# Attention and two feed-forward layers on one core: v's block sums on two column halves, and a new order of TensorE's work inside a step

## The chip, the cores and the metric

The kernel runs on one core of a Trainium2 chip. The metric is the device time of one execution in microseconds (us). Three executions of the kernel before gave 499.45 (median), 499.92 and 497.95 us. Engines are called by the names of the profile: PE is TensorE's matmuls, PEld its weight loads, DVE is VectorE, ACT is ScalarE, POOL is GpSimd, SP is the engine that issues the DMAs.

## The reference, cut to what matters

```python
# q, k, v: (2, 8, 768, 64) float32
block, window = 32, 16
k_sum = k.reshape(B, H, 24, 32, 64).max(axis=3)
v_sum = v.reshape(B, H, 24, 32, 64).mean(axis=3)
scores_l = where(|i - j| < 16, q @ k.T / 8, -1e9)
scores_s = q @ k_sum.T / 8 + log(32)
a = softmax(concat([scores_l, scores_s]))
attn = a @ concat([v, v_sum])
x = attn as (1536 tokens, 512)
h = x @ w_in;  x = (h * cos(h)) @ w_out           # 512 -> 2048 -> 512
h = x @ w_in2; x = layernorm(h * softmax(h)) * g_ln @ w_out2   # 512 -> 1024 -> 512
```

## The kernel before, in words

The 16 heads are worked in 8 pairs (n). A pair's 768 queries are cut into 12 tiles of 64, and 4 such tiles form a group G, so a pair has 3 groups and there are 24. Each tile of queries looks at a window of 96 keys and at the 24 block maxima of k, 120 columns in all. `kx` holds those columns, `qx` the scaled queries; both are copied by ACT out of one PSUM tile `qk` into which PE transposed k (L437) and q (L473).

The order of the work is written out by hand in `attention()`: a loop of 29 steps (24 groups and a lag of 5), and each engine does its instructions in just this order. In step s PE does, one after the other: some of the first feed-forward products h (`fill`, L234, in steps 15 to 18 and 20 to 28); the scores of group s+1 (`emit_s`, L501); the transposes of the softmax weights of group s-4 (`emit_t`, L538, tile `aps`); their products with v of group s-5 (`emit_av`, L556, tile `ops`); in steps 2, 5, 8, 11, 14 and 17 the transposes of the next k and q (`emit_k`, `emit_q`); in steps 1, 2, 4, 7, 10, 13, 16 and 19 the block sums of v of pairs 0 to 7 (`sum_v`, L419, tile `vsum`). Beside it, DVE does masking and maxima (L512), the softmax sums (L525, L526), the block maxima of k (L449) and the copies that lay k and q of two heads side by side (`pair_k`, `pair_q`, L375); POOL subtracts the maxima (L516) and scales by the sums (L531); ACT does the exponentials (L521), copies `aps` out as `at` (L546) and `ops` out into X (L570), `kx` and `qx`, scales `vsum` (L426, tile `vm`), and converts feed-forward weights. SP loads k, q, v and the weights, and places the scaled sums beside v, in partitions 96 to 119 of each tile of v (`place_vsum`, L430).

The block sums are a product on PE: a matrix of zeros and ones (a slice of `strip`, 96 rows by 24 columns) times a tile of v, accumulated over the 12 tiles into 24 rows of PSUM from row 96 on. The scores use 64 rows and 64 columns of PE's array for each of two heads. The transposes use the whole array (the profile shows 128*128 and 128*120), as do the products h. The products with v use 120 rows and, for the two heads in turn, the left and the right 64 columns.

After the loop the feed-forward layers follow: products y (L276) and h, 12 of 128 by 512 each, in turn, then the second layer.

Of the kernel before, what the change touches and what calls it, by code (L numbers as in the profile page):

```python
# [34 lines left out]
def fused_kernel(  # L35
# [299 lines left out]
    def attention():  # L335
        st = ExitStack()
        with st:
# [61 lines left out]
            strip = fix.tile([P, 2 * NS + 2 * (NS - 2)], F32, name="strip")  # L399
            FIRST, FINAL, MID = 0, NS, 2 * NS  # L400

            def block_columns():

                for at, row in ((FIRST, 0), (FINAL + NS - 2, WIN - QT), (MID + NS - 4, BAND)):
                    nc.vector.tensor_reduce(
                        out=strip[:, at:at + 2],
                        in_=ident[:, row:row + QT].rearrange("p (b k) -> p b k", k=BLOCK), op=ALU.add, axis=AX.X)

            def blocks_of(t):
                at = FIRST if t == 0 else FINAL if t == NT - 1 else MID + NS - 4 - 2 * t  # L410
                return strip[0:WIN, at:at + NS]

            def sum_v(n):

                o = (ps_h0 if n < 6 else ps_qk).tile(
                    [P, 512] if n < 6 else [P, 2, 2, S // 2], F32, tag="h" if n < 6 else "qk", name="vsum")
                o = o if n < 6 else o[:, 0, 0]
                for t in range(NT):
                    nc.tensor.matmul(  # L419
                        o[WIN:WIN + NS, 0:P], lhsT=blocks_of(t),  # L420
                        rhs=v_t[n][0:WIN, t].rearrange("p j d -> p (j d)"), start=(t == 0), stop=(t == NT - 1))
                vs_t[n] = o[WIN:WIN + NS, 0:P]

            def scale_v(n):
                m = io.tile([P, 2 * D], F32, tag="vm", name="vm")[WIN:WIN + NS]
# [3 lines left out]
            def place_vsum(n):  # L429
                nc.sync.dma_start(  # L430
                    out=v_t[n][WIN:WIN + NS].rearrange("p t j d -> p t (j d)"),
                    in_=vs_t.pop(n).unsqueeze(1).to_broadcast([NS, NT, 2 * D]))
# [163 lines left out]
            pair_k(1)  # L596
            pair_q(1)
            block_columns()
            emit_k(1)
            emit_q(1)  # L600
# [4 lines left out]
            for step in range(NGR + LA):  # L605
# [5 lines left out]
                fill(step)  # L611
                if step + 1 < NGR:
                    emit_s(step + 1)
                if LT <= step < NGR + LT:
                    emit_t(step - LT)
                if step >= LA:
                    emit_av(step - LA)
                if g == 2 and n + 2 < NPAIR:
                    emit_k(n + 2)
                    emit_q(n + 2)  # L620
                if step in VSUM_AT:
# [10 lines left out]
                if step < NGR:  # L632
# [335 lines left out]
```

## Time and profile before

| | |
|---|---|
| median of the three runs | 499.45 us |
| the profiled execution | 498.97 us |
| its span | 497.2 us |
| PE busy | 487.8 us (98% of the span) |
| ACT, DVE, POOL busy | 316.3, 299.9, 149.6 us |
| attention, until PE starts the products y | 0 to 109.3 us |
| share of the block sums (L419) in the chain that ended last | 4% |

The span is the time between the first and last instruction of the profiled execution; the 1.8 us to its own time lie around it. A busy PE is one that has an instruction in work: matmuls overlap, so a group of them is priced by the distance between its start and that of the next group. In the chain of waits each piece begins where the one before it released it, so its pieces give that distance directly. "x24" counts instructions: each float32 product with both operands in float32 shows as two, so 12 block sums are x24, 8 scores x16 and 8 products with v x16; transposes and products h show as one each.

### The profile page before, as it was taken

How to read it: one execution, taken by the hardware profiler on the slowest of the kernel's cores; microseconds unless marked ns; L12 is line 12 of the kernel's file. 1: busy time of each engine (PE TensorE's matmuls, PEld its weight loads, DVE VectorE, ACT ScalarE, POOL GpSimd, SP SyncE). 2: the span in 40 equal slices, each digit the busy share in tenths (PEclk: the TensorE clock that was granted, in tenths of full speed). 3: DMA queues.
4: the chain of work that ended last, by engine and by line, in shares of the span. 5: the costliest groups of instructions: out<-in, count | busy, mean ns of one | idle time of the engine just before them, and what ended most of it. 6: DMA issues, size and time to landing. Idle time of an engine off the chain costs nothing.

```text
span 497.2 us, 7856 instructions
## 1 busy us (share of the span) xinstructions
PE 487.8 (98%) x2938; PEld 400.7 (81%) x2938; DVE 299.9 (60%) x667; ACT 316.3 (64%) x540; POOL 149.6 (30%) x144
## 2 busy tenths in 40 slices
PE   6999999999999999999999999999999999999997
PEld 3888777778888888888888888888888788888886
DVE  3785775594444456465564645566476767676661
ACT  3467988673866865665566564678724876777621
POOL 1465986913422222232222221234600011110000
PEclk9999999999999999999999999999999999999999
DMA  8979852400223223322322330230001223223211
GB/s 218 233 207 267 228 130 73 140 2 0 86 87 119 90 84 105 108 86 86 116 94 84 101 112 2 85 100 28 0 1 42 81 74 96 70 64 65 63 42 44
DMA packets 58950, 46.17 MB, mean 93 GB/s; under 512 B 40352, under 2 KB 51232, under 8 KB 58912
## 3 DMA queue, kind: packets, MB, share of 16 engines
q1 hardware_dynamic: 58912, 45.67, 31.8%
q8 instruction: 23, 0.38, 0.3%
q14 instruction: 15, 0.12, 0.1%
HBM read 36.61 MB, written 3.15 MB: 80 GB/s over the span
## 4 chain that ended last, share of the span: by engine, by line
PE 92%; ACT 3%; DVE 2%; DMA 2%; SPq 0%; issue 0%; ACTq 0%
PE y L276 26%; PE h L234 26%; PE o L843 13%; PE h L729 13%; PE vsum L419 4%; PE sps L501 4%; PE aps L538 2%; PE ops L556 2%; DMA qt<-in_q_dram 2%; PE qk L473 1%; PE qk L437 1%; PE tp L777 1%; ACT kx L458 0%; ACT at L546 0%; ACT qx L487 0%
## 5 line engine op out<-in xcount | busy, mean ns | idle before, releaser
L234 PE MATMUL h<-xs,w 128*128 128x512 f32 x576 | 141.5, 392 | 0.4 <-ACT vm L426 0.4
L276 PE MATMUL y<-gs,w 128*128 128x512 f32 x576 | 138.1, 389 | 0.0
L276 PEld LDWEIGHTS y<-gs,w 128*128 128x128 f32 x576 | 108.0, 188 | 22.4
L234 PEld LDWEIGHTS h<-xs,w 128*128 128x128 f32 x576 | 107.2, 188 | 23.0 <-ACT vm L426 0.6
L187 POOL TENSOR_TENSOR w<-s,w 128x512 fp32r<-128x512 f32 x48 | 62.4, 1301 | 157.7 <-ACT w L186 134.7
L243 ACT ACTIVATE r<-h 128x512 int32<-128x512 f32 x48 | 28.7, 598 | 85.0 <-PE h L234 85.0
L248 DVE SCALAR_TENSOR_TENSOR r<-r,h 128x512 f32<-128x512 int32 x48 | 32.9, 686 | 66.8 <-ACT r L243 66.6
L843 PE MATMUL o<-w,ls 128*128 128x512 f32 (+1 forms) x312 | 67.8, 374 | 0.0
L729 PE MATMUL h<-w,xs 128*128 128x512 f32 x288 | 67.6, 390 | 0.0
L171 DVE SCALAR_TENSOR_TENSOR s<-raw 128x512 int32<-128x512 int32 x48 | 36.4, 758 | 51.0 <-ACT raw L164 43.7
L843 PEld LDWEIGHTS o<-w,ls 128*128 128x128 f32 x312 | 55.3, 188 | 10.7 <-DVE ls L819 0.4
L729 PEld LDWEIGHTS h<-w,xs 128*128 128x128 f32 x288 | 53.9, 188 | 11.1
L204 POOL TENSOR_TENSOR xs<-X,xs 128x512 fp32r<-128x512 f32 x22 | 30.7, 1405 | 35.4 <-ACT xs L203 35.4
L764 POOL TENSOR_TENSOR st<-st,mhalf 128x1 f32<-128x1 f32 x12 | 6.6, 552 | 110.1 <-DVE st L763 100.0
L253 ACT ACTIVATE r<-r,half_pi 128x512 f32<-128x512 f32 x48 | 34.4, 716 | 1.6 <-DVE r L248 1.6
L264 DVE TENSOR_TENSOR gs<-h,gs 128x512 fp32r<-128x512 f32 x48 | 32.6, 679 | 4.2 <-ACT gs L263 4.0
L516 POOL TENSOR_TENSOR sm<-sm,mx 128x480 f32<-128x480 f32 x24 | 25.7, 1070 | 27.1 <-DVE mx L512 27.1
L258 DVE TENSOR_TENSOR h<-h,r 128x512 f32<-128x512 f32 x48 | 32.8, 684 | 0.4 <-ACT r L253 0.4
L163 ACT ACTIVATE raw<-raw 128x512 f32<-128x512 f32 x48 | 31.9, 665 | 0.0
L164 ACT ACTIVATE raw<-raw 128x512 int32<-128x512 uint32 x48 | 31.8, 663 | 0.0
L186 ACT ACTIVATE w<-s 128x512 fp32r<-128x512 f32 x48 | 30.1, 627 | 1.3 <-DVE s L171 1.0
L746 ACT ACTIVATE e<-h,st 128x1024 f32<-128x1024 f32 (+1 forms) x13 | 13.6, 1049 | 26.3 <-DVE st L742 22.9
(79 smaller groups left out, 576.3 us busy)
## 6 DMA issues: line engine op xcount, KB each, us to landing
raw<-in_moe_w_in_dram SPq DMA_DIRECT2D x24, 512.0 KB, 3.5
raw<-in_moe_w_out_dram SPq DMA_DIRECT2D x24, 512.0 KB, 3.2
vt<-in_v_dram SPq DMA_DIRECT2D x16, 240.0 KB, 4.4
kt<-in_k_dram SPq DMA_DIRECT2D x8, 384.0 KB, 5.8
qt<-in_q_dram SPq DMA_DIRECT2D x8, 384.0 KB, 6.0
out_dram<-osb SPq DMA_DIRECT2D x11, 256.0 KB, 2.0
vt<-vm SPq DMA_DIRECT2D x8, 144.0 KB
vt<-in_v_dram SPq DMA_DIRECT2D x16, 48.0 KB, 3.7
```

The lines of the kernel that those rows point to most:

```text
L163: nc.scalar.activation(out=hw, in_=hw, func=AF.Prelu, scale=REBIAS, alpha=NEGATIVE)
L164: nc.scalar.activation(out=lw, in_=lw.bitcast(U32), func=AF.Copy, scale=TOP3)
L171: nc.vector.scalar_tensor_tensor(out=self.f32[i], in0=t[:, :, 1], scalar=3, in1=t[:, :, 0], op0=ALU.logical_shift_left, op1=ALU.bitwise_or)
L187: nc.gpsimd.tensor_tensor(out=w[:, 1, :], in0=f, in1=as32(w[:, 0, :]), op=ALU.subtract)
L234: nc.tensor.matmul(h, lhsT=w[:, a, f * P:(f + 1) * P], rhs=xs_of[tb, c][:, b_, :], start=(m == 0), stop=(m == 3 * KC - 1))
L248: nc.vector.scalar_tensor_tensor(out=r, in0=r.bitcast(I32), scalar=TWO_PI, in1=h_of[step], op0=ALU.mult, op1=ALU.subtract)
L253: nc.scalar.activation(out=r, in_=r, func=AF.Sin, scale=-1.0, bias=half_pi)
L258: nc.vector.tensor_tensor(out=h, in0=h, in1=r, op=ALU.mult)
L264: nc.vector.tensor_tensor(out=gs[:, 1, :], in0=r, in1=as32(gs[:, 0, :]), op=ALU.subtract)
L276: nc.tensor.matmul(y[e], lhsT=w[:, a, e * P:(e + 1) * P], rhs=gs[:, b_, :], start=(f == 0 and i == 0), stop=(f == GF - 1 and i == 2))
L729: nc.tensor.matmul(banks[n], lhsT=xs_of[NTB + t // TPB, c][:, a, t0:t0 + P], rhs=weights.done[w2i[c][n]][:, b_, :], start=(m == 0), stop=( ...
L843: nc.tensor.matmul(o, lhsT=ls_of[t][f // 4][:, a, s0:s0 + P], rhs=w[:, b_, cols], start=(f == 0 and i == 0), stop=(f == NF2 - 1 and i == 2))
```

## The change

`sum_v` now sums into two halves. Tiles 0 to 5 go through the left 64 columns of PE's array into rows 0 to 63 of PSUM, tiles 6 to 11 through the right 64 columns into rows 64 to 127, one product of each half in turn; 12 of the 64 columns of each half carry sums, the others are multiplied by zeros. `strip` is wider for that, `scale_v` scales 128 rows and not 24, and `place_vsum` issues two DMAs of 12 rows each in place of one of 24.

In a step, PE now does the scores, then `aps`, then the transposes of k and q, then `fill`, then the products with v, then the block sums. In step 0 the scores of group 1 come ahead of k and q of pair 1, and the maxima of group 0 ahead of `pair_k(1)`.

```diff
--- before.py
+++ after.py
@@ -396,40 +396,46 @@
                     )
                 v_t[n] = t
 
-            strip = fix.tile([P, 2 * NS + 2 * (NS - 2)], F32, name="strip")
-            FIRST, FINAL, MID = 0, NS, 2 * NS
+            HALF = NT // 2
+            FIRST, FINAL, MID = 0, D, 2 * D
+            strip = fix.tile([P, 3 * D + 2 * HALF], F32, name="strip")
 
             def block_columns():
 
-                for at, row in ((FIRST, 0), (FINAL + NS - 2, WIN - QT), (MID + NS - 4, BAND)):
+                for at, row in ((FIRST, 0), (FINAL + 2 * HALF - 2, WIN - QT), (MID + 2 * HALF, BAND)):
                     nc.vector.tensor_reduce(
                         out=strip[:, at:at + 2],
                         in_=ident[:, row:row + QT].rearrange("p (b k) -> p b k", k=BLOCK), op=ALU.add, axis=AX.X)
 
             def blocks_of(t):
-                at = FIRST if t == 0 else FINAL if t == NT - 1 else MID + NS - 4 - 2 * t
-                return strip[0:WIN, at:at + NS]
+                at = FIRST if t == 0 else FINAL if t == NT - 1 else MID + 2 * HALF - 2 * (t % HALF)
+                return strip[0:WIN, at:at + D]
 
             def sum_v(n):
 
                 o = (ps_h0 if n < 6 else ps_qk).tile(
                     [P, 512] if n < 6 else [P, 2, 2, S // 2], F32, tag="h" if n < 6 else "qk", name="vsum")
-                o = o if n < 6 else o[:, 0, 0]
-                for t in range(NT):
-                    nc.tensor.matmul(
-                        o[WIN:WIN + NS, 0:P], lhsT=blocks_of(t),
-                        rhs=v_t[n][0:WIN, t].rearrange("p j d -> p (j d)"), start=(t == 0), stop=(t == NT - 1))
-                vs_t[n] = o[WIN:WIN + NS, 0:P]
+                o = (o if n < 6 else o[:, 0, 0])[:, 0:P]
+                for t in range(HALF):
+                    for c in range(2):
+                        nc.tensor.matmul(
+                            o[D * c:D * c + D], lhsT=blocks_of(HALF * c + t),
+                            rhs=v_t[n][0:WIN, HALF * c + t].rearrange("p j d -> p (j d)"),
+                            start=(t == 0), stop=(t == HALF - 1))
+                vs_t[n] = o
 
             def scale_v(n):
-                m = io.tile([P, 2 * D], F32, tag="vm", name="vm")[WIN:WIN + NS]
+                m = io.tile([P, 2 * D], F32, tag="vm", name="vm")
                 nc.scalar.activation(out=m, in_=vs_t[n], func=AF.Copy, scale=1.0 / BLOCK)
                 vs_t[n] = m
 
             def place_vsum(n):
-                nc.sync.dma_start(
-                    out=v_t[n][WIN:WIN + NS].rearrange("p t j d -> p t (j d)"),
-                    in_=vs_t.pop(n).unsqueeze(1).to_broadcast([NS, NT, 2 * D]))
+                m = vs_t.pop(n)
+                for c in range(2):
+                    at = WIN + c * NS // 2
+                    nc.sync.dma_start(
+                        out=v_t[n][at:at + NS // 2].rearrange("p t j d -> p t (j d)"),
+                        in_=m[D * c:D * c + NS // 2].unsqueeze(1).to_broadcast([NS // 2, NT, 2 * D]))
 
             def transposed(t, even, odd):
 
@@ -593,11 +599,7 @@
             emit_qx(0)
             warm_up(3)
             emit_s(0)
-            pair_k(1)
-            pair_q(1)
             block_columns()
-            emit_k(1)
-            emit_q(1)
 
 
             LX, LN, LT, LA = 1, 2, 4, 5
@@ -608,16 +610,22 @@
                 ahead = n + 1 if g == 0 and n + 1 < NPAIR else 0
 
                 warm_up(IDLE[g] if step < min(FILL) else 0)
-                fill(step)
                 if step + 1 < NGR:
                     emit_s(step + 1)
+                if step == 0:
+                    emit_max(0)
+                    pair_k(1)
+                    pair_q(1)
+                    emit_k(1)
+                    emit_q(1)
                 if LT <= step < NGR + LT:
                     emit_t(step - LT)
-                if step >= LA:
-                    emit_av(step - LA)
                 if g == 2 and n + 2 < NPAIR:
                     emit_k(n + 2)
                     emit_q(n + 2)
+                fill(step)
+                if step >= LA:
+                    emit_av(step - LA)
                 if step in VSUM_AT:
                     sum_v(VSUM_AT[step])
 
@@ -629,7 +637,7 @@
                 if ahead and step:
                     emit_ksum(ahead)
                 weights.rebias()
-                if step < NGR:
+                if 0 < step < NGR:
                     emit_max(step)
                 if ahead and not step:
                     emit_ksum(ahead)
```

PE from the first scores on; `sps` are scores, `qk` the tile of the transposed k (from `kg`) and q (from `qg`). Before:

```order
L501 MATMUL sps<-kx,qx 64x120 x8
L437 MATMUL qk<-ident,kg 128x128 x6
L473 MATMUL qk<-ident,qg 128x128 x6
L501 MATMUL sps<-kx,qx 64x120 x16
L419 MATMUL vsum<-vt,strip 24x128 x12
```

With the change:

```order
L507 MATMUL sps<-kx,qx 64x120 x16
L443 MATMUL qk<-ident,kg 128x128 x6
L479 MATMUL qk<-ident,qg 128x128 x6
L507 MATMUL sps<-kx,qx 64x120 x8
L421 MATMUL vsum<-vt,strip 64x128 x12
```

The scores of group 1 moved ahead of k and q of pair 1; the block sums have 64 rows of output each and not 24.

PE from the transposes of k and q in step 14 to the block sums of step 16; `aps` are the transposed weights, `ops` the products with v, `h` the feed-forward products. Before:

```order
L437 MATMUL qk<-ident,kg 128x128 x6
L473 MATMUL qk<-ident,qg 128x128 x6
L234 MATMUL h<-xs,w 128x512 x3
L501 MATMUL sps<-kx,qx 64x120 x8
L538 MATMUL aps<-ident,sm_102 120x128 x4
L556 MATMUL ops<-at,vt 64x64 x8
L234 MATMUL h<-xs,w 128x512 x3
L501 MATMUL sps<-kx,qx 64x120 x8
L538 MATMUL aps<-ident,sm_97 120x128 x4
L556 MATMUL ops<-at,vt 64x64 x8
L419 MATMUL vsum<-vt,strip 24x128 x12
```

With the change:

```order
L443 MATMUL qk<-ident,kg 128x128 x6
L479 MATMUL qk<-ident,qg 128x128 x6
L562 MATMUL ops<-at,vt 64x64 x8
L507 MATMUL sps<-kx,qx 64x120 x8
L544 MATMUL aps<-ident,sm_102 120x128 x4
L234 MATMUL h<-xs,w 128x512 x3
L562 MATMUL ops<-at,vt 64x64 x8
L507 MATMUL sps<-kx,qx 64x120 x8
L544 MATMUL aps<-ident,sm_97 120x128 x4
L234 MATMUL h<-xs,w 128x512 x3
L562 MATMUL ops<-at,vt 64x64 x8
L421 MATMUL vsum<-vt,strip 64x128 x12
```

The transposes of k and q stand right behind `aps` and ahead of `ops`, and so do the products h, which led the step before.

## Rows read from the trace of the kernel before

**Rows 1.** The page, part 1: busy time, share of the span, instructions.

```profile
PE 487.8 (98%) x2938; PEld 400.7 (81%) x2938; DVE 299.9 (60%) x667; ACT 316.3 (64%) x540; POOL 149.6 (30%) x144
```

**Rows 2.** Busy time of each engine in stretches; first number: length of the stretch.

```profile
core 0: us, PE busy (x) PEld busy (x) DVE busy (x) ACT busy (x) POOL busy (x), PEclk, DMA share, GB/s
43.50:63.50 20.00, 19.41 (x267) 16.43 (x265) 14.17 (x57) 19.56 (x40) 16.98 (x15) 1.00 0.91 254
63.50:85.70 22.20, 21.38 (x256) 16.93 (x254) 14.10 (x62) 17.84 (x36) 17.00 (x16) 1.00 0.37 105
85.70:97.80 12.10, 12.06 (x144) 9.03 (x144) 8.71 (x44) 7.66 (x15) 11.70 (x12) 1.00 0.49 144
97.80:109.30 11.50, 10.74 (x121) 8.02 (x117) 9.61 (x19) 7.95 (x15) 1.89 (x3) 1.00 0.01 2
109.30:497.20 387.90, 384.72 (x1730) 318.95 (x1728) 225.72 (x375) 241.46 (x396) 83.31 (x70) 1.00 0.24 71
```

**Rows 3.** Chain of waits, attention: start us, us until the next piece, what.

```profile
12.74 1.79 PE sps L501 x32
14.52 2.73 PE vsum L419 x24
17.25 0.97 PE sps L501 x16
...
24.78 2.73 PE vsum L419 x24
...
29.06 0.61 PE ops L556 x16
29.68 0.81 PE qk L437 x6
30.48 0.66 PE qk L473 x6
...
63.86 0.70 PE h L234 x3
...
66.73 0.89 PE h L234 x3
```

**Rows 4.** Instructions that read v's tiles: weight loads, ns min/median/max.

```profile
L556 PEld LDWEIGHTS ops<-at,vt x384: 132/138/138, 29.0 to 109.1; 120*64 120x64 f32 x192
L419 PEld LDWEIGHTS vsum<-vt,strip x192: 98/103/103, 14.5 to 85.0; 96*24 96x24 f32 x192
```

**Rows 5.** Timeline of DVE at the start: start us, us, instruction.

```profile
9.04 0.55 DVE L375 COPY kg<-kt 128x768 f32<-128x768 f32 x1
...
10.35 0.28 DVE L512 CUSTOM_DVE_ANT_0 sm<-sps,mask 128x120 f32<-128x120 f32 x1 [0.38 <-PE sps L501]
...
11.16 0.08 DVE L512 DVE_READ_ACCUMULATOR2_ANT mx<- 128x1 f32 x1
```

**Rows 6.** Timeline of SP's issues: v of pair 2 (last), sums placed.

```profile
18.67 1.72 SPq L393 DMA_DIRECT2D vt<-in_v_dram  x1
20.49 3.04 SPq L430 DMA_DIRECT2D vt<-vm  x2
```

**Rows 7.** Loads of v issued between 18.6 and 19 us: landing.

```profile
DMA to landing us min/median/max: 4.4/4.4/4.4
```

**Rows 8.** Timeline of ACT in step 12, first piece.

```profile
52.09 0.60 ACT L546 ACTIVATE at<-aps 120x512 f32<-120x512 f32 x1
```

**Rows 9.** Timeline of PE: next aps, and late starts (in brackets).

```profile
53.41 0.65 PE L538 MATMUL aps<-ident,sm 128*120 128x128 f32 x4
...
82.58 2.80 PE L419 MATMUL vsum<-vt,strip 96*24 96x128 f32 x24 [0.50 <-ACT qx L487]
85.74 1.20 PE L234 MATMUL h<-xs,w 128*128 128x512 f32 x4 [0.36 <-ACT vm L426]
...
108.65 0.69 PE L556 MATMUL ops<-at,vt 120*64 120x64 f32 x16 [0.76 <-DVE X L568]
```

## The prediction

> **What bounds the kernel now.** I read the page first: PE is busy 98% of the span [rows 1]. Then the stretches, to see whether that holds where the change acts. From 109.3 us on, the feed-forward layers, PE is busy 384.72 of 387.90 us; the change touches nothing there, so whatever attention gains shifts that part as a whole, and what is to be found is how much earlier the products y can start than at 109.3. In attention PE is nearly full too, but between 43.5 and 63.5 us ACT is busy 19.56 of 20.00 us, between 85.7 and 97.8 POOL 11.70 of 12.10, and behind that DVE 9.61 of 11.50 [rows 2]. So PE sets the pace up to about 43 us, and later it shares it. The granted clock is full (1.00) in all of these stretches, so no piece below is one at half speed. Last, the chain of waits gives the price of each group of PE's work, from one start to the next [rows 3].
>
> **The block sums.** One pair's take 2.73 us, 24 instructions of 128 columns: 114 ns each, 0.89 ns a column. All 24 go through the same columns of the array. What work costs that alternates between two parts of the array is seen twice. 32 instructions of the scores take 1.79 us and 16 take 0.97, so 16 more cost 0.82, 51 ns each for 120 columns: 0.43 ns a column. The products with v, 16 instructions of 64 columns that alternate between the left and the right half just as the new sums do, take 0.61 us: 0.60 ns a column with their entrance (below), 0.45 without [rows 3]. So the new sums cost 24 x 128 x 0.43 = 1.31 us; at most 1.83 if the 0.60 holds for them; and 2.73 if the halves don't overlap. I take 1.31: the 120 columns of the scores are nearest to 128 in length, and the products with v come to the same pace in the same geometry.
>
> [...] Both halves use the same rows. [...]
>
> **Changes of kind on PE.** A group that follows another use of the array costs more than one that follows its own kind: scores 0.97 against 0.82, six transposes 0.81 behind products with v and 0.66 behind transposes, three products h 0.89 behind products with v and 0.70 behind transposes [rows 3]. So an entrance costs 0.15 to 0.19 us.
> - Block sums behind products with v are now of the same kind and have none: 1.31. In steps 1, 2 and 4 they follow something else: 1.46. Saved: 3 x 1.27 + 5 x 1.42 = 10.9.
> - k's transposes now follow aps in steps 5, 8, 11, 14 and 17: 5 x 0.15 = 0.75.
> - Products h now follow aps. In steps 16, 17 and 20 to 23 that saves 0.19 each, 1.14. In 15 and 18 they stood behind q's transposes already. In 24 to 27, which have no scores, aps takes over the entrance that h loses; step 28 has no aps. Nothing there.
>
> **Start.** The scores of group 1 (0.82) move into time in which PE waited for q. But the maxima of group 0 now come ahead of pair_k(1) on DVE: they end at 11.24, the copy of 0.55 at 11.8 [rows 5], then k's transposes 0.81, q's 0.66, scores 0.97 [rows 3]: the first block sums start at 14.2, not 14.52. Gain 0.33, not 0.82.
>
> In all PE has 10.9 + 0.75 + 1.14 + 0.33 = 13.1 us less to do before y. What of it stays, by stages:
>
> **To step 9 (41.8 us).** 0.33, three sums at 1.27, one at 1.42, two of 0.15 for k: 5.86. Against it stands v of pair 2. SP issues its last piece at 18.67, in a row of issues without a gap [rows 6], and it lands 4.4 later [rows 7], at 23.07. Its sums, at 24.78 before, could start at 24.78 - 0.33 - 2 x 1.27 = 21.9 and will wait 1.16. Gain 4.7. Placing the sums takes one issue more a pair: the two issues at 20.49 end at 23.53, partly because the second waits for vm; four, if each costs the half of 3.04, end at 26.6 at the latest, and the loads of the next k, q and v begin up to 3 us later. k and q are read three steps after they are loaded, so I price this at nothing and leave the rest to the range.
>
> **Steps 9 to 14.** PE saves two sums and two entrances, 3.14. ACT has 0.44 of idle time in 20 us [rows 2], and its work stays (vm has as many columns as before, so it costs the same). PE can run ahead of ACT only as far as copies have slack: in step 12 the copy of aps ends at 52.69 and PE needs its place at 53.41 [rows 8, 9], 0.72. So 0.44 + 0.72, about 1.2. Bounds: 0.44 and 3.14.
>
> **Steps 15 to 19.** Two sums 2.84, one k 0.15, two h 0.38, and the 0.36 that h of step 20 waited for vm [rows 9], since scores and aps now stand ahead of it: 3.73. ACT needs 17.84 of the 18.5 us that are left [rows 2]. It fits barely; the 0.50 that the last sums wait for qx [rows 9] shows ACT ending last there, so I take 3.5.
>
> **Steps 20 to 23.** Four entrances, 0.76, but POOL has only 0.40 of idle time in this stretch [rows 2]: 0.4.
>
> **Steps 24 to 28.** DVE is the last here: PE waits 0.76 for its copy of ops [rows 9]. Nothing gained, that wait stays.
>
> Sum: 4.7 + 1.2 + 3.5 + 0.4 = 9.8 us of the 13.1. The profiled execution (498.97 us, span 497.2) becomes 489.2; the median of the runs lies 0.48 above that execution, so I forecast **489.7 us**. Its own range is a gain of 7.5 to 12 us, 487.5 to 492.
>
> **Rivals.**
> 1. *ACT and POOL hold more.* Steps 9 to 14 give their 0.44 and no slack, 15 to 19 give 1.5 because ACT enters them late, 20 to 23 nothing: 4.7 + 0.44 + 1.5 = 6.6, 492.8 us. For it: ACT at 98% for 20 us. Against it: ACT is busy only 17.84 of 22.20 in the next stretch and can catch up. The sums at 1.83 instead of 1.31, 8 x 0.52 = 4.2 less, would end near the same place, at 493.9.
> 2. *Nothing is returned.* All 13.1 are kept: 486.4. Against it stand the waits named above.
> 3. *The change doesn't do what it says:* the halves alternate but don't overlap, and the sums stay at 2.73. Then only entrances, the start and the 0.36 remain, 0.75 + 1.14 + 0.33 + 0.36 less what POOL holds: about 2.2, 497.3, within 0.5% (2.5 us, about what a measurement of this kernel can tell from no change). Against it: 38 ns for each product with v.
> 4. *Slower, through the weight loads of the sums.* Each load now brings 64 columns and not 24. Loads of 64 columns take 132 to 138 ns, those of 24 took 98 to 103 [rows 4]. If each load has to wait until the other half's product is through, the loads set the pace: 24 x 0.138 = 3.31, 0.58 more than now, 8 times, less the 2.2 of rival 3: 2.4 slower, 501.9; more, if load and product follow each other fully. It decides from 2.73 + 2.2/8 = 3.0 us a pair on, 125 ns an instruction. For it: 114 ns now lie close above the 103 of a load, as if loads set the pace already. Against it: the same products with v.
>
> **How the numbers follow.** Forecast 0.74; rival 1 with the dearer sums 0.13; rival 2 0.02; rival 3 0.07; rival 4 0.04. The range leaves out rivals 3 and 4, most of rival 2 and the far end of rival 1: 486.8 to 493.5. Faster by over 0.5%: forecast, rivals 1 and 2, and a little of rival 3: 0.90; within: most of rival 3 and the near part of 4: 0.07; slower: 0.03.
>
> **What would show it.** In the profile after: block sums of 1.3 to 1.5 us a pair, and no longer 4% of the chain; products h at 0.70 and k's transposes at 0.66 behind aps; a wait of the third sums for v; ACT without idle time over some 18 us, with PE waiting for at or for maxima in steps 11 to 15; y starting near 99.5. I am wrong if the sums stay above 1.9, if y starts after 104, or if the part behind y changes its length by more than 1 us.

## The result, and the profile after

The changed kernel takes 493.67 us (median of 13 runs, 491.32 to 496.64), the kernel before beside it 498.88 (13 runs, 497.63 to 500.09): a ratio of 0.9893, 95% interval 0.9871 to 0.9915. It is faster by 5.2 us; forecast were 489.7 and a gain of 9.8, and the result lies 0.2 us above the upper end of the forecast's range, 486.8 to 493.5. The profiled execution took 492.56 us, its span is 490.8, and PE is busy 477.8 of that; before it was 487.8 [rows 1].

First the price of the sums, in the chain of waits of attention (start us, us until the next piece, what):

```profile
20.04 1.46 PE vsum L421 x24
...
26.88 0.66 PE qk L443 x6
...
33.14 1.31 PE vsum L421 x24
...
62.22 0.70 PE h L234 x3
```

The sums of a pair fell from 2.73 [rows 3] to 1.46 behind another use of the array and 1.31 behind products with v; the transposes of k behind `aps` cost 0.66, the products h behind `aps` 0.70. All four are the forecast prices to the hundredth; behind a wait of PE the transposes cost 0.71.

Then where the time is, by the timeline of PE. These rows start the stages of the prediction (first block sums, step 9, step 15, step 20, step 24, products y):

```profile
15.05 1.53 PE L421 MATMUL vsum<-vt,strip 96*64 96x128 f32 x24
37.86 1.04 PE L507 MATMUL sps<-kx,qx 64*64 64x120 f32 x16
60.60 1.04 PE L507 MATMUL sps<-kx,qx 64*64 64x120 f32 x16
79.15 1.04 PE L507 MATMUL sps<-kx,qx 64*64 64x120 f32 x16
91.39 0.65 PE L544 MATMUL aps<-ident,sm 128*120 128x128 f32 x4
102.89 0.50 PE L276 MATMUL y<-gs,w 128*128 128x512 f32 x1
```

The same starts in other runs give the table that the rest of this text goes by (us; the last row is an experiment told below, one placing transfer instead of two). In the old order a step begins with the products h, in the new one with the scores or, from step 23 on, with `aps`; each length is from one step's first group to the other's. The forecast's 4.7 to step 9 stands in two columns, 0.33 and 4.4.

| kernel | first sums at | to step 9 | 9 to 14 | 15 to 19 | 20 to 23 | 24 to y | first sums to y |
|---|---|---|---|---|---|---|---|
| before | 14.45 | 27.31 | 21.86 | 22.12 | 12.07 | 11.46 | 94.82 |
| after | 15.05 | 22.81 | 22.74 | 18.55 | 12.24 | 11.50 | 87.84 |
| gain, measured | -0.6 | 4.5 | -0.9 | 3.6 | -0.2 | 0.0 | 7.0 |
| gain, forecast | 0.33 | 4.4 | 1.2 | 3.5 | 0.4 | 0 | 9.5 |
| one place | 14.48 | 22.79 | 22.09 | 18.54 | 12.26 | 11.51 | 87.19 |

Two stages did what was forecast. Steps 9 to 14 gave a loss and not a gain, and steps 20 to 23 nothing. The part behind y is unchanged, 387.9 us with PE busy 384.7, as in [rows 2]. These are PE's waits in steps 9 to 14 and in the last sums (end of the line: length and releaser):

```profile
45.58 0.62 PE L544 MATMUL aps<-ident,sm 128*120 128x128 f32 x4 [1.04 <-ACT at L552]
52.03 1.04 PE L507 MATMUL sps<-kx,qx 64*64 64x120 f32 x16 [1.51 <-DVE mx L518]
57.43 0.88 PE L443 MATMUL qk<-ident,kg 128*128 128x128 f32 x6 [0.30 <-DVE kg L375]
58.98 0.87 PE L479 MATMUL qk<-ident,qg 128*128 128x128 f32 x6 [0.68 <-DVE qg L375]
77.62 1.60 PE L421 MATMUL vsum<-vt,strip 96*64 96x128 f32 x24 [0.49 <-ACT qx L493]
```

The first four, in steps 11, 13 and 14, add up to 3.5 us. In the kernel before PE had one wait there, for maxima of DVE as well:

```profile
55.27 1.04 PE L501 MATMUL sps<-kx,qx 64*64 64x120 f32 x16 [0.59 <-DVE mx L512]
```

By the starts of the steps, steps 10 and 13 (the sums) became 1.4 us shorter each, and steps 11, 12 and 14 became 1.15, 0.93 and 1.63 us longer: 0.9 more in all. Why ACT's `at` is late in step 11 stands in ACT's timeline just before it, and in SP's before that:

```profile
43.74 0.67 ACT L163 ACTIVATE raw<-raw 128x512 f32<-128x512 f32 x1 [0.56 <-DMA raw<-in_moe_w_in_dram]
```

```profile
35.05 2.95 SPq L393 DMA_DIRECT2D vt<-in_v_dram  x1
38.10 1.67 SPq L436 DMA_DIRECT2D vt<-vm  x2
39.82 1.50 SPq L139 DMA_DIRECT2D raw<-in_moe_w_in_dram  x3
```

ACT waits for the first feed-forward weights. SP issues them at 39.82, in the kernel before at 39.89, though PE is 3.9 us ahead by then (step 9 begins at 37.86 and not 41.76): the two placing transfers ahead of them take 1.67 us where one took 0.83, and the loads of v ahead of those up to 2.95 each. The prediction had priced the second transfer at nothing.

### The profile page after: what moved, and what is told of

The parts are those of the page before. It is cut to its first block, busy times and chain, and to the rows that moved or that the text cites. A ratio compares the mean times of both kernels' runs of the same rounds, so it can differ in the third digit from the quotient of the medians.

```text
span 490.8 us, 7868 instructions
## 1 busy us (share of the span) xinstructions
PE 477.8 (97%) x2938; PEld 392.4 (80%) x2938; DVE 299.8 (61%) x667; ACT 314.1 (64%) x540; POOL 149.8 (31%) x144
## 4 chain that ended last, share of the span: by engine, by line
PE 87%; ACT 3%; POOL 3%; DVE 3%; DMA 2%; issue 1%; SPq 0%; ACTq 0%; POOLq 0%
PE y L276 27%; PE h L234 26%; PE o L851 13%; PE h L737 13%; PE sps L507 2%; PE ops L562 1%; PE aps L544 1%; POOL sm L522 1%; PE vsum L421 1%; DMA qt<-in_q_dram 1%; DMA raw<-in_moe_w_in_dram 1%; POOL sm L537 1%; POOL w L187 1%; ACT kx L464 1%; PE qk L443 1%
## 5 line engine op out<-in xcount | busy, mean ns | idle before, releaser
L171 DVE SCALAR_TENSOR_TENSOR s<-raw 128x512 int32<-128x512 int32 x48 | 36.7, 764 | 52.3 <-ACT raw L164 44.1
L754 ACT ACTIVATE e<-h,st 128x1024 f32<-128x1024 f32 (+1 forms) x13 | 13.6, 1049 | 26.3 <-DVE st L750 22.9
```

Of the source, the lines that this page charges most:

```text
L171: nc.vector.scalar_tensor_tensor(out=self.f32[i], in0=t[:, :, 1], scalar=3, in1=t[:, :, 0], op0=ALU.logical_shift_left, op1=ALU.bitwise_or)
```

## The experiments

The theories: **Q**, the second placing transfer of each pair lengthens SP's queue, so weights and v come late, and PE waits for that; **P**, the order inside a step or the work of one engine (ACT, DVE, POOL) holds PE in steps 9 to 23; **C**, PE's granted clock falls in some runs (the means of the changed kernel's runs lie between 0.992 and 1.000) and costs the rest. Medians are given with the ratio to the kernel before on the same chip and its 95% interval.

### The same kernel again, and each half of the change alone

No edit:

> The changed kernel once more, to see the spread of its runs and the granted clock of each, beside runs of the kernel before. Theory C (the time that differs between runs is clock: where PE waits, the clock sometimes falls for a few us): the runs at a mean clock of 1.000 take 491 to 492.5 us, those at 0.993 to 0.997 take 493 to 496.5, and the kernel before, which waits less, stays at 1.000 in nearly all its runs, 498 to 500. Theory D (the spread is not clock but the transfers): the kernel before shows as many runs below 1.000, and time and clock go apart. The median of all runs: 493.7, give or take 0.8.

492.61 us, 0.9884 (0.9859 to 0.9910): the gain is confirmed, with a median 1.1 below what was expected. The mean clock sorts the runs only in part: at 0.997 they took 492.3 to 495.2, and 8 of the 23 runs of the kernel before lay below 1.000, where theory C wanted nearly none. The sums alone, with the old order and start:

```diff
 new sum_v, strip, scale_v, place_vsum (two transfers)
 fill(step); emit_s; emit_t; emit_av; emit_k, emit_q; sum_v     # as before
```

> Sums on two halves, with the order inside a step and at the start as before. By the prediction's own sum the order is worth 0.33 + 0.75 + 1.14 + 0.36 of PE time, so this kernel loses up to 2.2 us against the change: 495.5 to 496. Theory A (the new order gives its entrances back, because the products with v now wait behind k, q and h, and ACT's copy of ops with them, where ACT is the bound): no slower than the change, 492.5 to 494, and ACT's idle time before its copy of ops in steps 14 to 17 is gone.

496.82 us, 0.9953 (0.9929 to 0.9977): a gain of 2.3 us, less than either range wanted. The order and the start alone:

```diff
 old sum_v, strip, place_vsum
-fill(step); emit_s; emit_t; emit_av; emit_k, emit_q; sum_v
+emit_s; emit_t; emit_k, emit_q; fill(step); emit_av; sum_v
```

> The new order with the block sums as before (24 columns, one placing DMA). By the prediction's sum: 2.2 us faster than before, 496.7. Theory A: PE saves its entrances, but in the stretch where ACT is the bound the products with v come later: 0 to 1 us faster, 498 to 499.

497.13 us, 0.9966 (0.9952 to 0.9981): a gain of 1.7 us, near the prediction's own sum; its lengths are 27.07, 22.08, 21.13, 11.42 and 11.50. Of the 10.9 us that the sums save on PE only 2.3 appear, and both parts together give 1.2 to 1.8 us more than their sum of 4.0. Something is lost with the sums alone that the new order partly avoids.

### One placing transfer instead of two

The left half's sums are put in rows 52 to 63 and the right half's in 64 to 75, so that one transfer places all 24 rows:

```diff
-                m = vs_t.pop(n)
-                for c in range(2):
-                    at = WIN + c * NS // 2
-                    nc.sync.dma_start(
-                        out=v_t[n][at:at + NS // 2]...,
-                        in_=m[D * c:D * c + NS // 2]...)
+                nc.sync.dma_start(
+                    out=v_t[n][WIN:WIN + NS]...,
+                    in_=vs_t.pop(n)[LEAD:LEAD + NS]...)      # LEAD = 52
```

> The change, with the sums of the left half written to rows 52 to 63 and those of the right half to rows 64 to 75, so that one DMA places all 24 rows. Theory Q (the second placing DMA fills SP's queue, and the first weights come late: ACT waits 0.56 for them at 43.2 us): the first weights are issued about 0.8 us earlier, that wait goes, and the kernel is 0.5 to 1.2 us faster than the change: 492.5 to 493.2. If the queue only moves its waits elsewhere: the same as the change within 0.4.

491.76 us, 0.9858 (0.9840 to 0.9875), 7.1 us faster than before, and faster than theory Q expected. SP's and PE's timelines of this run, to be held against those above:

```profile
34.08 2.06 SPq L393 DMA_DIRECT2D vt<-in_v_dram  x1
36.23 0.82 SPq L435 DMA_DIRECT2D vt<-vm  x1
37.10 1.68 SPq L139 DMA_DIRECT2D raw<-in_moe_w_in_dram  x3
```

```profile
44.33 0.62 PE L543 MATMUL aps<-ident,sm 128*120 128x128 f32 x4 [0.37 <-ACT at L551]
```

The weights are issued 2.7 us earlier (2.1 if counted from the first sums), ACT no longer waits for them, and the wait for `at` falls from 1.04 to 0.37; steps 9 to 14 take 22.09 and not 22.74. The same edit on the version with the sums alone:

> The old order and start, the sums on two halves, but with the rows chosen so that one transfer places all 24. With two transfers this was 0.9953 of before. Theory Q (the second transfer of each pair lengthens SP's queue, so v and the first weights land late): the queue cost the changed kernel 0.9 to 1.9 us, so without it 0.992 to 0.9935, 495.0 to 496.0 us, y starting 1 to 2 us earlier than the 107.3 of the two-transfer version. Theory O (in the old order ACT and DVE hold PE, whatever SP does): 0.995, y at 107. The prediction's own sum (10.9 us saved, nothing of it due to the order) would be 0.985.

493.43 us, 0.9883 (0.9862 to 0.9903), more than theory Q said: the second transfer cost that version 3.5 us of its median (0.9953 to 0.9883; the intervals lie apart). ACT's timeline of the version with two transfers shows how:

```profile
44.78 0.65 ACT L163 ACTIVATE raw<-raw 128x512 f32<-128x512 f32 x1 [1.71 <-DMA raw<-in_moe_w_in_dram]
```

In the version with one transfer that wait is gone, steps 9 to 14 take 21.30 instead of 22.98, and 20 to 23 take 12.09 instead of 13.59 (the clock, below). By the ratios the sums alone are then worth 5.8 us and the order alone 1.7, and the 7.1 of both together is about their sum: what had looked like help between the two was the queue. The transfer by itself, in the kernel before:

```diff
-                nc.sync.dma_start(out=v_t[n][WIN:WIN + NS]..., in_=vs_t.pop(n)...)
+                m = vs_t.pop(n)
+                for c in range(2):
+                    nc.sync.dma_start(out=..., in_=m[c * NS // 2:(c + 1) * NS // 2]...)   # 12 rows each
```

> The kernel before, with nothing changed but that each pair's 24 sums are placed by two transfers of 12 rows instead of one of 24. Theory Q: slower by 1 to 2 us, 1.002 to 1.004 of before, with SP's issues for v and the first weights later. Theory L (the queue matters only where PE is ahead of the loads, and in the kernel before PE is not): 1.000, within 0.1%.

499.00 us, 0.9999 (0.9988 to 1.0010), and all five lengths as before within 0.03 us. Theory Q in its plain form falls, rival L stands: one issue more a pair cost nothing in this kernel, where PE is not ahead of the loads. It got its price through the change's own gain.

### The start

One placing transfer, and the maxima of group 0 again behind pair 1's copies and transposes:

```diff
+            pair_k(1)
+            pair_q(1)
             block_columns()
+            emit_k(1)
+            emit_q(1)
...
-                if step == 0:
-                    emit_max(0)
-                    pair_k(1)
...
```

> The changed kernel with one placing transfer (0.9858 of before), but group 0's maxima again behind pair 1's copies and transposes. The prediction's term for the start, 0.33 us: 0.9865 of before, and the first block sums 0.33 us later. Rival: the start is worth nothing, because the wait for pair 1's qx takes the place of the one removed: 0.9858, within 0.1%, or better.

491.78 us, 0.9852 (0.9832 to 0.9872), no different. From the first sums to step 9 this version takes 22.28 against 22.79: in the new start the scores of step 2 wait 0.96 us for pair 1's `qx`, which takes the place of what was removed. The first sums themselves start anywhere from 13.6 to 16.1 us in the profiled executions of this study, and the first transposes of q ahead of them, which wait for its load by way of ACT's copy, at 6.7 to 8.0 us and in 0.9 to 1.5 us, so a term of 0.33 can't be read from there. Counted from the scores of group 0, where these run at full pace or near it, the first sums follow after 4.99 to 5.15 us in the profiles with the new start and after 4.46 to 5.57 in those with the old one: the new start gains nothing that shows.

### What holds PE from step 9 to step 23

Each of the next kernels has one placing transfer. `at` of groups 6 to 10 moved from ACT to DVE:

```diff
-                if G >= DVE_AT:
+                if G >= DVE_AT or 6 <= G < 11:
```

> The changed kernel with one placing transfer (0.9858 of before), and besides the copy of aps (0.59 us each on ACT) of groups 6 to 10 on DVE, steps 10 to 14. Theory S (ACT's work holds PE between 37 and 60 us, which is why steps 9 to 14 gave nothing): 1 to 2 us more, 0.982 to 0.984, and step 16's scores 1 to 2 us earlier against step 10's. Rival T (DVE, busy 16.9 of 23 us there and in turn waiting for ACT, becomes the bound): 0.9858 or slower, and PE's waits for maxima grow.

494.75 us, 0.9908 (0.9891 to 0.9925), slower; steps 9 to 14 take 23.14 and 15 to 19 take 19.92. Theory S's gain does not come, and PE's wait for maxima in step 13 grows from 1.52 to 1.87, as rival T had it; but the work only went to another engine, so this does not yet clear ACT. DVE's order is the reason to look at: its joining of weight words (L171) waits for ACT's words, and behind it stand the copies of k and q and the maxima. In step 14 of the version with one transfer:

```profile
54.37 1.29 DVE L171 SCALAR_TENSOR_TENSOR s<-raw 128x512 int32<-128x512 int32 x1 [2.01 <-ACT raw L164]
```

So the copies were put ahead of it:

```diff
+                if g == 1 and n + 2 < NPAIR:
+                    pair_k(n + 2)
+                    pair_q(n + 2)
                 weights.finish()
```

> The changed kernel with one placing transfer (0.9858 and 0.9852 of before in its two forms), and besides DVE's copies of pair n+2's k and q ahead of, not behind, the joining of weight words that waits for ACT. Theory S2 (steps 9 to 14 gave only 0.65 us because DVE stands in the queue for ACT's weight words with the copies that PE's transposes wait for): sps of step 15 another 1 to 2 us earlier, no waits of PE for kg and qg, 0.982 to 0.984. Rival A (ACT's work as such fills the stretch): 0.985, and the waits move to at or to maxima.

492.37 us, 0.9870 (0.9853 to 0.9887). The waits for the copies went and steps 9 to 14 fell to 20.58, 1.5 less, as theory S2 had it. But steps 15 to 19 rose from 18.54 to 20.17, so its 0.982 to 0.984 did not come: the gain went one stage on and no further. What PE met there, on PE and DVE:

```profile
63.59 1.04 PE L506 MATMUL sps<-kx,qx 64*64 64x120 f32 x16 [1.51 <-DVE mx L517]
```

```profile
59.60 1.50 DVE L171 SCALAR_TENSOR_TENSOR s<-raw 128x512 int32<-128x512 int32 x1 [0.76 <-POOL w L187]
```

PE waits for maxima, and those stand behind weight words that now wait for POOL. POOL's scaling of groups 17 to 19 moved to DVE, and this with the edit before:

```diff
-                (nc.vector if G >= DVE_NORM else nc.gpsimd).tensor_tensor(
+                (nc.vector if 17 <= G < 20 else nc.gpsimd).tensor_tensor(
```

> The changed kernel with one placing transfer, and the products with the reciprocal sums of groups 17 to 19 (1.4 us each on POOL) on DVE, steps 19 to 21. Theory G (POOL, busy 12.0 of 12.0 us between 78 and 90 us, takes back 1.4 us of what steps 15 to 19 gain): 0.983 to 0.984, y 0.7 to 1.4 us earlier than 101.67. Rival D (DVE is the next bound there, its joined words and maxima come later): 0.985 to 0.987, y no earlier.

> Both edits of the two kernels before on top of one placing transfer. If the two holds are in different stretches, their gains add: 0.980 to 0.982, 489 to 490 us. If what one stretch gives is taken back by the other, no more than the better of the two.

492.86 us, 0.9882 (0.9865 to 0.9899), and 493.14, 0.9887 (0.9872 to 0.9902). Steps 20 to 23 rose from 12.26 to 13.1 in both: as rival D had it, DVE is the next to hold there, and it costs a little more than rival D's range.

Moving work only moved the wait, so three kernels left work of one engine out:

```diff
-                nc.gpsimd.tensor_tensor(out=w[:, 1, :], ...)
+                if i >= 2 * KC:
+                    nc.gpsimd.tensor_tensor(out=w[:, 1, :], ...)
```

> The changed kernel with one placing transfer, without the low parts of the first 8 weight tiles (8 subtractions of 1.27 us on POOL, 10.2 us in all, left out; the feed-forward products that would use them take the high part instead, so PE's work is the same). From the scores of step 9 to those of step 20 that kernel takes 40.6 us, PE's work being 37.0. If POOL sets the pace there: 37.5 to 38.5 us, and y about 2.5 us or more earlier. If ACT or DVE does: 40.2 to 40.6. If the ring of all three does: in between, 39 to 40.

```diff
-                if LX <= step < NGR + LX:
+                if LX <= step < NGR + LX and not 9 <= step - LX < 20:
                     emit_exp(step - LX)
```

> The changed kernel with one placing transfer, without the exponentials of groups 9 to 19 (11 of 0.49 us on ACT, 5.4 us, left out). If ACT sets the pace between the scores of step 9 and those of step 20: 37.5 to 38.5 us instead of 40.6. If POOL or DVE does: 40.2 to 40.6. If the ring does: 39 to 40.

```diff
             def emit_sum(G):
+                if 8 <= G < 19:
+                    sum_t[G] = ones
+                    return
```

> The changed kernel with one placing transfer, without the row sums and reciprocals of groups 8 to 18 (11 of 0.7 us on DVE, some 8 us, left out; the products use ones). If DVE sets the pace between the scores of step 9 and those of step 20: 37.5 to 38.5 us instead of 40.6. If ACT or POOL does: 40.2 to 40.6. If the ring does: 39 to 40.

The scores of step 9 to those of step 20 take 40.58, 40.70 and 41.94 us, against 40.63 with all the work in (the third has a clock of 0.76 and 0.67 from 56 to 62 us, and its three groups of PE there take 1.3 us more than the same groups with all the work in); the medians are 492.05, 491.91 and 491.75 us, ratios 0.9870, 0.9863 and 0.9860. No one engine's amount of work sets these stages. Without the exponentials steps 9 to 14 did become shorter, 21.43 instead of 22.09, but steps 15 to 19 longer by as much, 19.27 instead of 18.54. Steps 20 to 23 became shorter without the low parts, 11.60 instead of 12.26, and without the exponentials, 11.73. The windows of that stage, after and there (length; busy us of PE, PEld, DVE, ACT, POOL; clock, DMA share, GB/s):

```profile
79.15:91.39 12.24, 11.62 (x145) 8.86 (x144) 9.66 (x44) 8.83 (x19) 12.24 (x13) 1.00 0.50 142
```

```profile
77.05:88.65 11.60, 11.47 (x145) 8.86 (x144) 8.90 (x44) 8.91 (x19) 7.65 (x8) 1.00 0.51 150
```

POOL has no idle time there in the changed kernel; with 5 instructions of POOL fewer in the stretch PE is busy 11.47 of 11.60. This speaks for POOL as what holds steps 20 to 23, as the prediction said. But with the order alone the stage took 11.42 us, and POOL was busy for all of them with 12 instructions while PE never waited: what counts seems to be the work that POOL still has when PE enters the stage. Last, the copies first and the low parts left out together:

```diff
+pair_k, pair_q ahead of weights.finish()
+if i >= 2 * KC: nc.gpsimd.tensor_tensor(...)
```

> One placing transfer, DVE's copies of k and q ahead of the joining of weight words, and the low parts of the first 8 weight tiles left out (10.2 us off POOL; the feed-forward products take the high part in their place, PE's work is the same). Each edit alone left the stretch from the scores of step 9 to those of step 20 at 40.6 to 40.8 us. Theory R (two chains in turn: with the copies first the wait moves to POOL's low parts, which DVE's joining of words then waits for): 38 to 39.5 us. Rival V (what holds there is neither): 40.3 to 40.8.

Steps 15 to 19 take 18.58 again. That fits theory R, which gave the wait of 1.51 to POOL, but does not show it: steps 9 to 14 take 22.44, with one wait of 2.12 us for maxima and slower work of PE behind it (the scores there took 1.86 us and not 1.04; the run's mean clock is 0.995), so PE enters steps 15 to 19 as late as without either edit. The sum is 41.0, within neither theory's numbers. The median is 491.24 us, 0.9860 (0.9830 to 0.9890). PE's own work from the scores of step 9 to those of step 20 is 37.0 of 40.6 us. The 3.6 between seem to hang on the order in which ACT, DVE and POOL hand weight words, copies and maxima to each other. That is argued from the waits, and which hand-over would have to go first is open.

### The clock

Of the changed kernel's 13 runs four had a mean granted clock of 1.000 and took 491.3 to 492.6 us; nine had 0.992 to 0.997 and took 492.0 to 496.6, 494.3 on average against 491.95. The profile of the same kernel again caught such a run. ACT's and PE's timelines, and the windows around them (clock is the third number from the end):

```profile
45.40 0.65 ACT L163 ACTIVATE raw<-raw 128x512 f32<-128x512 f32 x1 [2.05 <-DMA raw<-in_moe_w_in_dram]
```

```profile
47.22 1.08 PE L544 MATMUL aps<-ident,sm 128*120 128x128 f32 x4 [2.51 <-ACT at L552]
48.09 1.49 PE L443 MATMUL qk<-ident,kg 128*128 128x128 f32 x6
```

```profile
42.00:45.00 3.00, 2.71 (x56) 2.30 (x50) 0.00 (x0) 1.35 (x3) 1.25 (x2) 1.00 1.00 365
45.00:48.00 3.00, 0.78 (x4) 0.81 (x5) 1.38 (x3) 2.60 (x7) 0.05 (x1) 0.74 1.04 343
48.00:51.00 3.00, 3.00 (x18) 2.67 (x18) 2.63 (x12) 2.65 (x6) 3.00 (x3) 0.50 1.02 258
51.00:54.00 3.00, 3.00 (x36) 2.60 (x34) 2.97 (x13) 1.39 (x3) 3.00 (x3) 0.63 0.65 128
```

In this run the weights came later still: ACT waited 2.05 us for them and not 0.56. PE stood 2.51 us for `at`, the granted clock went to 0.50, and the transposes of k took 1.28 us to the next start and not 0.66; steps 9 to 14 take 24.25 and not 22.74. So part of what the lower clock costs comes from the queue too. Idle products in two of the waits were to keep PE at work:

```diff
+                warm_up(4 if step == 13 else 0)
                 if step + 1 < NGR:
                     emit_s(step + 1)
+                warm_up(4 if step == 11 else 0)
```

> The changed kernel, with two placing transfers as it is, and four idle products of 512 columns (0.21 us each at the full clock) ahead of aps in step 11 and four ahead of the scores in step 13, where PE waited 1.04 and 1.51 us. Theory C (those waits are what the lower granted clock follows in some runs: 9 of the 13 runs, and 4 of the 6 later ones, had a mean clock below 1.000 and took up to 496.6): nearly all runs at 1.000 or 0.999, 492.0 median, none above 493.5. Rival N (the clock has another cause): the same spread of clocks as before, median 492.6 to 494.2.

496.51 us over all nine runs, 0.9937 (0.9915 to 0.9959) without the longest of them; eight of the nine were below 1.000. The edit did the reverse of what was meant: the idle products write to the place in PSUM that the block sums of step 10 hold until ACT has copied them, and PE waited 3.9 us for that, with the clock at 0.50 behind it:

```profile
46.00:49.00 3.00, 0.15 (x1) 0.10 (x1) 1.60 (x4) 2.83 (x7) 0.29 (x1) 0.97 1.04 353
49.00:52.00 3.00, 2.78 (x10) 2.00 (x10) 2.65 (x13) 2.32 (x5) 3.00 (x3) 0.50 0.93 204
```

As an experiment on a longer wait it speaks for theory C. Two cleaner ones put a wait into the version with one placing transfer, ahead of `aps` and ahead of the scores of step 11:

```diff
+                warm_up(1 if step == 11 else 0)
                 if LT <= step < NGR + LT:
                     emit_t(step - LT)
```

> The changed kernel with one placing transfer (five runs, all at a mean granted clock of 1.000), and one idle product ahead of aps in step 11, whose place in PSUM comes free only when ACT has copied the block sums of step 10: PE waits there some 2 to 4 us. Theory C (the lower clock follows a long wait of PE): most runs below 0.998, the profile with PEclk near 0.5 behind that wait, and the time longer by the wait and by another 1.5 to 3 us: 494.5 to 497.5. Rival N: the clock stays at 1.000 in most runs, and the time grows by no more than the wait, 491.8 to 494.5.

491.88 us, 0.9864 (0.9843 to 0.9885): the wait came out at 1.25 us and replaced others, so neither theory was tried.

```diff
-                warm_up(IDLE[g] if step < min(FILL) else 0)
+                warm_up(1 if step == 11 else 0)
```

> The changed kernel with one placing transfer, and one idle product ahead of the scores of step 11, waiting for ACT's copy of the block sums of step 10: PE waits there about 2.3 us. Without it 12 of 15 runs of the plain one-transfer kernels' kind had a mean granted clock of 0.999 to 1.000 and none was below 0.995. Theory C (the lower clock follows long waits of PE): several runs at 0.993 or below, with time 2 to 4 us above 491.8. Rival N: clocks as without it, time 491.8 to 493.5.

492.76 us, 0.9892 (0.9867 to 0.9917), with a wait of 2.19 us. Three of six runs had a clock of 0.997 and took 493.3 to 495.3, three had 1.000 and took 492.0 to 492.2; none was at 0.993 or below, where theory C wanted several. In its profile (493.75 us, 0.997) the clock stays at 1.00 behind the wait. It is low elsewhere, ahead of the first sums, where PE had waited 2.35 us for the first q:

```profile
8.00:12.00 4.00, 4.00 (x27) 2.83 (x29) 1.43 (x5) 1.83 (x4) 0.00 (x0) 0.57 0.96 225
```

The profile with `at` on DVE (0.996) has the same, 0.57 there behind a wait of 2.23 us, and 1.00 after it. So a run's mean of 0.995 to 0.997 does not tell whether the clock fell in attention's later waits or at the start, behind a wait that comes ahead of all that was changed. The two versions with the sums alone show as well that the wait alone does not decide it: both wait 1.13 and 1.4 us around step 20, and the clock then falls to 0.77 and 0.66 in the one with two transfers and stays at 1.00 in the other. The version with less work on DVE fell behind waits of 0.4 to 0.8 us only. So the falls stand behind waits of PE, but a wait's length doesn't tell whether one comes. What decides stays open. What is shown is where they are frequent: at 0.993 or below were 5 of the 19 runs of the changed kernel, 6 of 12 with the sums alone and two transfers, 4 of 9 with the idle products; none of the 43 runs of the versions with one transfer that do all of the work, and none of the 24 of the order alone and of the kernel before with two transfers. But 3 of the 9 runs of the two versions without POOL's low parts were there too (0.992, 0.993 and 0.992), with one transfer, so the second transfer is not the only way to it.

## Why the prediction was right or wrong

**The price of the sums: right.** 1.31 and 1.46 us, 55 ns an instruction, by the pace of scores and products with v. Both halves use the same 96 rows, and 24 weight loads of 137 ns each, 3.3 us together, stand beside the 1.31: the products of the two halves overlap, and the loads don't set the pace. Rivals 3 and 4 fall.

**Entrances: right** by the same rows: 0.66 for k, 0.70 for three products h.

**To step 9: the size right by luck**, 4.5 measured from the first sums on against 4.4. The prediction took off 1.16 for a wait of the third sums for v. The profile has no such wait; in its place the scores of step 2 wait 0.96 for pair 1's `qx`, which the prediction did not have. In the profile of the same kernel again both waits come, 0.96 and 0.85, and the gain is 3.5.

**The start, 0.33: not shown.** The start of the first sums varies by 2.5 us between executions, and the edit that undid this part changed no median. The step left out that pair 1's `qx` becomes late in its turn.

**"Placing takes one issue more a pair ... I price this at nothing": wrong.** The reason given was that k and q are read three steps after they are loaded. They are, but that is the wrong cover: behind k, q and v in the same queue stand the first feed-forward weights. Taken away, the second transfer gives back 0.65 us in steps 9 to 14 of the profile and 1.3 to 1.7 us of the median (0.9893 and 0.9884 against 0.9858; these intervals overlap a little, so the size is not sharp; those of the version with the sums alone, 0.9953 against 0.9883, don't). The median can have more than the profile because late weights can lengthen PE's wait and the clock can fall behind it, as in the profile of the same kernel again (a wait of 2.51 us, then a clock of 0.50). In the kernel before it costs nothing (0.9999), so a price taken there would have been zero as well; it had to be judged at the pace after the change, with SP's issues held and PE's drawn 4.5 us forward.

**Steps 9 to 14, +1.2: wrong, -0.9.** 0.65 of the 2.1 missed is the queue. The rest comes from treating ACT as one engine with 0.44 of idle time and 0.72 of slack. That its copy of `vm` would cost the same held: 277 ns for 128 rows (median), 270 for 24 before. What PE waits for is not ACT's amount of work: between 42.5 and 61 us ACT is busy only 16.48 of 18.50, not without idle time as the prediction's sign had it, and 5.4 us off ACT gave 0.66 here and took it back in the next stage. PE waits for maxima that stand on DVE behind weight words, sums and block maxima (1.5), and for the copies of k and q behind weight words (0.30 and 0.68). The 0.59 that PE waited for maxima in step 13 of the kernel before was a sign of this, and the prediction left it out. With the copies first this stage gives 1.3, and the next gives it back; which hand-over sets the two together stays open. Rival 1 had the direction, and its 492.8 is nearer to the result than the forecast, but by another mechanism than its own. The 493.9 named beside it is nearest by luck: it stood on dearer sums.

**Steps 15 to 19, +3.5: right**, 3.6: the wait for `vm` is gone and the one of 0.49 for `qx` stays, as forecast. The order is needed for it: with the sums alone, one transfer, the stage takes 21.58, with both 18.54.

**Steps 20 to 23, +0.4: wrong by 0.6.** What the runs show speaks for POOL as the bound, and it stays busy the whole stage, but 13 of its instructions now fall into the stage and not 12 [rows 2], and fill the 0.40 that were to be given.

**The median.** The profiled execution gains 6.4 and the median 5.2. The four runs at 1.000 gain 6.9; the rest is in the nine below. Where in these the clock fell is not recorded, and the kernel before has runs at 0.995 to 0.997 too. That the clock was full in all stretches of the kernel before was read as settled for the kernel after; with waits of 1 to 2.5 us in it, it is not.

## What to carry to other kernels

A cost that is hidden before a change is hidden by the pace before it: an extra transfer that was free in the old kernel cost 1.3 to 3.5 us of the median once PE ran ahead of the loads. So for each queue ask what stands behind the new entry, up to the last reader, at the new pace. And in a stage in which three engines hand work to each other in fixed orders, the idle time of the busiest one did not give the price; the waits point at the hand-overs. Here the best kernel is the changed one with its sums in neighbouring rows and one placing transfer: 491.76 us, 0.9858 of before, in either form of the start.

## What the runs showed of the hardware

Products that alternate between the left and the right 64 columns, with the same 96 rows and a new weight load each, go at 55 ns for 128 columns, though each load takes 137 ns; in one place of 24 columns they took 114. No run has 64 columns in one half alone, so the width is not tried by itself.

DVE's copies of k and q took longer where they started inside an instruction of POOL. The copy of q (0.55 us where no instruction of POOL is in work as it starts) took 1.64 in step 14 of the version with one transfer, and it ended 0.4 us after POOL's product did:

```profile
56.05 1.64 DVE L375 COPY qg<-qt 128x768 f32<-128x768 f32 x1
```

```profile
55.69 1.59 POOL L204 TENSOR_TENSOR xs<-X,xs 128x512 fp32r<-128x512 f32 x1 [0.57 <-ACT xs L203]
```

In the profiles before and after, each of the 11 of these copies that start inside an instruction of POOL ends 0.4 us behind it; what holds them is not shown. By an estimate from these numbers, without the delay of 1.1 us (1.64 less 0.55) the copy would have ended at 56.6 us, before PE was ready for q at 57.06 (its wait of 0.68 ends at 57.74); so that wait hangs on it.

Inside attention a wait of PE of more than 2 us was followed by slower work of PE in three profiles (2.51 and 3.9 us, with a clock of 0.50 behind them, and 2.12 us, with scores of 1.86 us and not 1.04 behind it) and not in two others (2.19 in both, 1.00 behind it), so one profile can't show whether a kernel has this loss. The mean clock of all runs shows how often the clock is low, but not where.
